# Dividing by the sum of dispatch weights behind the experts, with the token logits, norms, late weight tiles and gates in other places: one fused kernel (windowed attention, soft mixture of experts, routed mixture of experts) on one core

## The chip, the core and the metric

The kernel runs on one core of a Trainium2 chip. The core has a matrix engine (TensorE; PE in the views, and PEld for its weight loads), three elementwise engines (VectorE or DVE, ScalarE or ACT, GpSimd or POOL) and SyncE (SP), whose instruction queue starts nearly all transfers between HBM and the on-chip memory. Each engine works through its own queue strictly in order, and engines wait for each other by semaphores. Matrix products are written into eight PSUM banks of 128 x 512 fp32 values, from which ACT and DVE copy them on.

The metric is the device time of one execution in microseconds. For a comparison with the kernel before, several rounds are run on the same chip.

## What is computed

The reference chains three parts over 3,072 tokens of width 512. Cut to what matters here:

```python
# 1. attention with 4 sink keys and a window of 128 -> x [3072, 512]
# 2. soft mixture of experts: 8 experts, 4 slots each (32 slots)
logits = x @ phi
d = np.exp(logits - logits.max(0)); d /= d.sum(0) + 1e-09        # over tokens, per slot
slot_input = (d.T @ x).reshape(8, 4, 512)
for e in range(8):
    slot_out[e] = np.maximum(slot_input[e] @ w1[e], 0.0) @ w2[e]
c = np.exp(logits - logits.max(1)); c /= c.sum(1) + 1e-09         # over slots, per token
x = c @ slot_out.reshape(32, 512)
# 3. routed mixture of experts: every token goes to the best of 8 by cosine
logits = xn @ en.T / tau          # xn, en: rows divided by their norms
out = gate * (np.maximum(x @ w1[best], 0.0) @ w2[best])
```

Because `relu` passes a positive factor through, a positive division of `slot_input` by `d.sum(0)` can be done before the two weight products of an expert or behind them.

## The kernel before, in words

**Attention** (lines 201 to 520). 48 units (16 head pairs, 3 units each) are put into one order by a table of numbers (`KEYS`). The change does not touch it. Its last products are the token logits of the last head pair (`emit_f`, L369), added into `lt_all` (96 rows: 3 groups of 32 slots; 4 batches; 256 tokens) by DVE at L390.

**The mixture** (`mixture`, from L616) is a set of generators, each cut into steps. What order they run in stands in the string `ORDER` (L1410 and following): every name in it is one step of one generator, and each step puts its instructions at the end of its engine's queue. The names that matter:

- `wgt`, `scale`, `shift`: the maximum over the last batch and the rest, exponentials `e_sb`, their transpose `et_sb`, the common shift `a96`, the weight `wgt`, the running sum `s_run`. `scale` multiplies sum and weight, adds the 3 groups with a product against `rr96` (L700), and makes `rw = rsel * wgt / (sum + 1e-9)` (L702 to L705).
- `sum0`, `sum1` (two column halves of d.T @ x, L713, gathered into `si_acc` at L716); `in0`, `in1`: `si_acc` times `rw` (L723), copied into `sit`, the transposed slot inputs (L725).
- `f00` to `f13`: first weight products, `f<group of 4 experts><quarter of 512 inputs>` (L834); `t00` to `t11` relu and transposes; `v0`, `v1` second products (L858), `tu0`, `tu1` their transposes into `sot` and `ems` (L865 to L883).
- `tok0`, `tok1`: token logits back to rows of tokens, `c_tok` (L751 to L772; half of them by a copy `lt0` in the tile of `xtok`); `comb` their softmax over slots; `tot` the sum of c over tokens; `p0` to `p5` and `s0` to `s5` split and transpose c into `cs_t` (`cstack`).
- `norm`: 1 / (norm * tau) of the 8 expert embeddings (L731 to L746).
- `ch`: the likeliest expert, from `sot` x `ems`, then x `ccol`, then a maximum (L891 to L904). With its index SP starts the loads of that expert's two weights (L993, L995). `route`, `logit`, `cmp`, `gate`: routing logits, maxima, norms and gates of all tokens. `q0` to `q3` (L1021): slot outputs times the chosen expert's first weight.
- `T` (L1192) with `c0` to `c47`: 48 products, and on each a test that counts signs, 28 on ACT (L1201) and 20 on DVE (L1203). `ca`, `cb`, `e`, `gat`, `row`, `fetch` then pick the few hidden units whose sign is mixed and fetch their rows of the second weight by an indirect DMA. `D` (L1228) full products for 2 token tiles, `y2` to `y23` (L1375) four products for each of the other 22, `st` the scaled copies and stores (L1234, L1236).
- `K` and `J` are products whose result nobody reads. They keep PE busy: 25 `K` and 19 `J`, all 25 `K` ahead of `f00`.

**Weights and their tiles.** The 16 blocks of 2 MB expert weights go through the tiles `w0` to `w8` and a few others. Blocks 0 to 3 feed `f00` to `f03`, 4 to 7 feed `v0`, 8 to 11 feed `f10` to `f13`, 12 to 15 feed `v1`. Blocks 0 to 10 are loaded during attention. Blocks 11 to 15 each wait in SP's queue until an older tile has been read:

```python
for i in range(11, 16):
    load_w(i, wp, f"w{max(0, i - 11) + (i > 11)}", split=(i == 15))   # w0, w2, w3, w4, w5
```

Later tiles reuse the same tags: `cstack` in `w1`, `room` (scratch of `cmp` and `gate`) and then `sel` in `w3`, `junk` (scratch of the sign tests) in `w4`, `w2h` in `w5`.

## Time and profile before

| what | us |
|---|---|
| runs of the kernel (three) | 283.7, 287.44, 288.27; median 287.44 |
| the profiled execution, whole | 286.0 |
| its span, from the first to the last instruction | 284.3 |
| PE busy | 265.9 (94%) |
| DVE busy | 194.3 (68%) |
| ACT busy | 192.7 (68%) |
| POOL busy | 161.4 (57%) |

The profile is one execution. Its span leaves out 1.7 us around the first and the last instruction. A busy share is an average over stages that have different limits, so the stages are read one by one, from views that list instructions in order of time with what ended the idle time ahead of them. The granted clock of PE is given as a share of its full 2.4 GHz, so 1.00 is the upper and 0.50 the lower of its two levels.

### The profile page before, as it was taken

What the parts mean: (1) busy time and instruction counts of PE and PEld (TensorE: products, weight loads), DVE (VectorE), ACT (ScalarE), POOL (GpSimd) and SP (SyncE); (2) the same over time, 40 slices, a digit from 0 to 9 for tenths busy, and PEclk for the clock granted to TensorE, in tenths of its full rate; (3) what the DMA queues carried; (4) which work ended last, traced back from release to release, by engine and by line L of the source; (5) the groups of instructions that cost most, each with busy time, mean ns of one, the idle gap of its engine ahead of it and who ended that gap; (6) DMA issues with size and microseconds to landing.
All of it is one profiled execution on the core that took longest, in us unless ns stands there. A gap on an engine that the chain in (4) does not pass through costs nothing. (4 is left out here: it accounts for less than half of the span.)

```text
span 284.3 us, 8839 instructions
## 1 busy us (share of the span) xinstructions
PE 265.9 (94%) x3252; PEld 167.8 (59%) x3252; DVE 194.3 (68%) x573; ACT 192.7 (68%) x676; POOL 161.4 (57%) x375
## 2 busy tenths in 40 slices
PE   7987999979999989999999999989999999999992
PEld 5654666545666655666656563324277766577881
DVE  6887888988888988789986141383423999656420
ACT  2677989869799697898978510241124899775982
POOL 3488999978789788899798430001200999020000
PEclk9999999999999999999999999999999999999999
DMA  7939976198463795976807497999309400024785
GB/s 211 330 130 395 387 282 207 35 419 347 137 261 115 265 417 187 322 262 225 327 1 297 142 425 262 403 348 367 129 25 397 170 1 1 2 74 110 265 324 195
DMA packets 15053, 65.37 MB, mean 230 GB/s; under 512 B 2720, under 2 KB 2976, under 8 KB 11424
## 3 DMA queue, kind: packets, MB, share of 16 engines
q1 hardware_dynamic: 13456, 63.77, 60.1%
q10 hardware_dynamic: 1392, 0.48, 0.8%
q8 instruction: 27, 0.44, 0.6%
q0 software_dynamic: 160, 0.52, 0.6%
q14 instruction: 18, 0.15, 0.1%
HBM read 58.48 MB, written 6.29 MB: 228 GB/s over the span
## 5 line engine op out<-in xcount | busy, mean ns | idle before, releaser
L261 ACT ACTIVATE pr<-sc,nm 128x132 f32<-128x132 f32 x192 | 68.7, 375 | 8.4 <-DVE rs L266 3.4
L271 POOL TENSOR_TENSOR pr<-pr,rs 128x528 f32<-128x528 f32 x48 | 51.5, 1073 | 22.4 <-DVE rs L267 17.3
L261 ACT ACTIVATION_READ_ACCUMULATOR pr<-sc,nm 128x1 f32 x192 | 40.3, 210 | 0.0
L224 PE MATMUL sc<-qk 64*32 64x164 f32 (+4 forms) x1536 | 36.8, 295 | 0.3 <-ACT pr L261 0.2
L239 DVE COPY_PREDICATED sc<-t_le_q,sc 128x512 f32<-128x512 uint32 x48 | 33.1, 689 | 3.5 <-PE sc L224 2.0
L295 ACT ACTIVATE raw<-m 128x512 f32<-128x512 f32 x48 | 29.0, 604 | 7.9 <-PE xb L324 4.3
L247 DVE TENSOR_REDUCE sc<-sc 128x4 f32<-128x528 f32 x48 | 33.7, 703 | 0.8
L290 PE MATMUL m<-ident,pr 128*128 128x128 f32 x192 | 30.2, 279 | 4.3 <-ACT xtok L379 2.1
L301 POOL TENSOR_SCALAR_AFFINE_SELECT pt<-raw 128x512 f32<-128x512 f32 x48 | 30.6, 639 | 1.9 <-ACT raw L295 1.9
L345 PE MATMUL xa<-pt,v 128*64 128x256 f32 (+1 forms) x256 | 30.3, 360 | 0.0
L290 PEld LDWEIGHTS m<-ident,pr 128*128 128x128 f32 x192 | 21.4, 141 | 12.5 <-POOL pr L271 3.5
L224 PEld LDWEIGHTS sc<-qk 64*32 64x32 f32 x1536 | 21.4, 107 | 10.8 <-issue 4.7
L813 POOL CAST scr<-scr 128x256 fp32r<-128x256 f32 x6 | 2.4, 401 | 35.1 <-DVE scr L809 34.4
L345 PEld LDWEIGHTS xa<-pt,v 128*64 128x64 f32 x256 | 15.4, 136 | 8.4 <-issue 4.6
L308 POOL TENSOR_SCALAR_AFFINE_SELECT pt<-raw 128x256 f32<-128x256 f32 x48 | 19.6, 409 | 0.0
L345 PE MATMUL xb<-pt,v 128*64 128x128 f32 (+1 forms) x192 | 18.9, 314 | 0.0
L1169 POOL TENSOR_TENSOR w2h<-w2t,ones 128x512 fp32r<-128x512 f32 x8 | 8.4, 1056 | 16.3 <-DMA w2t<-in_m2w_dram 16.3
L379 ACT ACTIVATE xtok<-m 128x512 f32<-128x512 f32 (+1 forms) x32 | 15.7, 499 | 2.0 <-PE m L362 1.7
L1375 PE MATMUL b<-w2c,hm 128*128 128x512 f32 x54 | 17.0, 397 | 0.0
L362 PE MATMUL m<-ident,xt 128*128 128x128 f32 x96 | 15.9, 276 | 0.0
L345 PEld LDWEIGHTS xb<-pt,v 128*64 128x64 f32 x192 | 11.6, 136 | 7.3 <-POOL st L281 2.5
L1234 ACT ACTIVATE ot<-b,gsel 128x512 f32<-128x512 f32 x19 | 12.4, 687 | 3.3 <-PE b L1228 1.4
(354 smaller groups left out, 572.7 us busy)
## 6 DMA issues: line engine op xcount, KB each, us to landing
w<-in_m1w_dram SPq DMA_DIRECT2D x19, 1024.0 KB, 7.7
qk<-in_qkv_dram SPq DMA_DIRECT2D x15, 780.0 KB, 4.2
w<-in_m1w_dram SPq DMA_DIRECT2D x4, 2048.0 KB, 9.0
v<-in_qkv_dram SPq DMA_DIRECT2D x16, 448.0 KB, 5.0
out_dram<-ot SPq DMA_DIRECT2D x20, 256.0 KB, 3.4
x<-in_m1w_dram SPq DMA_DIRECT2D x4, 1024.0 KB, 8.1
w1t<-in_m2w_dram SPq DMA_DIRECT2D x4, 512.0 KB, 5.6
w2t<-in_m2w_dram SPq DMA_DIRECT2D x4, 512.0 KB, 8.3
```

Of the source, the lines that this page charges most:

```text
L224: pe.matmul(sc[r0:r0 + 32, h, o + lo:o + hi], lhsT=lhsT, rhs=qk[hp:hp + 64, k0 + lo:k0 + hi], start=True, stop=True)
L239: dve.copy_predicated(mv[:, :, :, 0:128], mk.to_broadcast([128, 2, 2, 128]), bv[:, :, :, 124:252])
L247: dve.tensor_reduce(mx, mv[:, :, :, 0:UW], axis=X, op=ALU.max, negate=True)
L261: act.activation(out=pr[:, h, i2, :], in_=mv[:, h, i2, 0:UW], func=AF.Exp, bias=nm[:, h, i2:i2 + 1], scale=0.125, accum_out=sm[:, h, i2, 0:1])
L271: pool.tensor_tensor(out=pr, in0=pr, in1=sm.rearrange("p h (i o) -> p h i o", o=1).to_broadcast([128, 2, 2, UW]), op=ALU.mult)
L290: pe.transpose(ps[:, h, i2, :], pr[:, h, i2, 0:128], ident)
L295: act.activation(out=raw, in_=tp_t.pop(u), func=AF.Copy)
L301: pool.affine_select(out=pt[:, :, :, 0, :], in_=raw_t[u], pattern=[[0, 2], [0, 2], [1, 128]], compare_op=ALU.is_ge, fill=0.0, base=0, chan ...
L308: pool.affine_select(out=pt_t[u][:, :, 0, 1, :], in_=raw_t[u][:, :, 1, :], pattern=[[0, 2], [-1, 128]], compare_op=ALU.is_gt, fill=0.0, ba ...
L345: pe.matmul(o[64 * h:64 * h + 64, c0:c0 + 128 * (l1 - l0)], lhsT=v[:, j, h, :], rhs=mv[:, h, 128 * l0:128 * l1], start=False, stop=last, s ...
L362: pe.transpose(ps[:, 128 * t:128 * t + 128], xt[:, 128 * (t0 + t):128 * (t0 + t) + 128], ident)
L1375: pe.matmul(y, lhsT=a, rhs=b, start=(k == 0), stop=(k == 3))
```

## The change

1. **Sum divided out later.** `rw` is now `rsel * wgt` alone. The sum is brought into the layout of the experts' outputs by two products against a table `rsl` (filled by POOL) and inverted into `rinv`; `tu0` and `tu1` multiply by it while they copy the outputs out of PSUM. `rr96` goes.
2. **Token logits and norms ahead.** `tok0`, `tok1` and the first steps of `norm` stand ahead of the first weight product. The token logits no longer need the copy `lt0`. `sit` is copied by ACT instead of DVE.
3. **Choice of the expert** by one group of eight products: c's sum over tokens is spread to 128 rows (`ccb`), multiplied into the outputs and summed on DVE (`mtm`, `mt`), instead of two products with a copy between.
4. **Other tiles for late loads**: blocks 11 to 15 go to `w0` to `w4` (before `w0, w2, w3, w4, w5`), `cstack` to `w5`, `w2h` to `w1`, `room` beside `junk` in `w4`.
5. **Gates behind the sign tests**: three of the five `gate` steps move from between the tests to behind the last `e6`, the other two behind `gat`.
6. **Warm-ups**: 25 `K` become 13 (6 ahead of `f00`), 19 `J` become 12. `s0` and `s1` move behind `v1`.
7. **The last token tile** is multiplied, copied and stored in two halves of 256 columns.

The diff, cut (the new `ORDER` is shown by its rows below; the parts for inputs of other kinds are left out):

```diff
-    rr96 = const.tile([96, 3, NS], F32, name="rr96")
...
+        rsl = sb.tile([96, 2, 4, NS], F32, name="rsl")
+        rinv = sb.tile([128, 2], F32, name="rinv")
+        ccb = sb.tile([128, NS], F32, name="ccb")
+        mtm = sb.tile([128, 4, 16], F32, name="mtm")
+        mt = sb.tile([128, 2, 4], F32, name="mt")
...
+            dve.tensor_scalar(out=rw, in0=rsel, scalar1=wgt, scalar2=None, op0=ALU.mult)
...
-            pe.matmul(tp[0:96, 256:257], lhsT=rr96.rearrange("p g s -> p (g s)"), rhs=s96, start=True, stop=True)
-            yield
-            dve.tensor_scalar(out=s96, in0=tp[0:96, 256:257], scalar1=1e-9, scalar2=None, op0=ALU.add)
+            for g in range(2):
+                pe.matmul(tp[:, g:g + 1], lhsT=rsl[:, g].rearrange("p j s -> p (j s)"), rhs=s96, start=True, stop=True)
+            yield
+            dve.tensor_scalar(out=rinv, in0=tp[:, 0:2], scalar1=1e-9, scalar2=None, op0=ALU.add)
             give(tp)
-            dve.reciprocal(out=s96, in_=s96)
-            dve.tensor_scalar(out=rw, in0=rsel, scalar1=wgt, scalar2=s96, op0=ALU.mult, op1=ALU.mult)
+            dve.reciprocal(out=rinv, in_=rinv)
...
-            dve.tensor_copy(sit[:, 2 * n:2 * n + 2, :, 0:SPE], ps[:, 2 * NS * n:2 * NS * n + 2 * NS].rearrange("p (c e s) -> p c e s", c=2, e=E))
+            act.activation(out=sit[:, 2 * n:2 * n + 2, :, 0:SPE], in_=ps[:, 2 * NS * n:2 * NS * n + 2 * NS].rearrange("p (c e s) -> p c e s", c=2, e=E), func=AF.Copy)
...
-            for k in range(2):
-                pe.transpose(tp[:, 32 * k:32 * k + 32], lt0[:, k, 128 * b2:128 * b2 + 128], ident[0:32, 0:32])
+            for b in range(2):
+                for k in range(2):
+                    pe.matmul(tp[64 * b:64 * b + 64, 32 * k:32 * k + 32], lhsT=lt_all[:, 2 * b2 + b, 64 * k:64 * k + 64], rhs=ident[0:96, 0:32], start=True, stop=True)
...
-            act.activation(out=so_sb[:, 0:256], in_=so[:, 0:256], func=AF.Copy)
+            act.activation(out=so_sb[:, 0:256], in_=so[:, 0:256], func=AF.Copy, scale=rinv[:, g:g + 1])
...
-            for c in range(4):
-                pe.matmul(ps[0:NS, 0:E], lhsT=sot[:, c], rhs=ems[:, c, 0:E], start=(c == 0), stop=(c == 3))
-            yield
-            dve.tensor_copy(e32[:, 0:E], ps[0:NS, 0:E])
...
-            pe.matmul(ps[0:1, 0:E], lhsT=ccol, rhs=e32[:, 0:E], start=True, stop=True)
+            for g in range(2):
+                for c in range(4):
+                    pe.matmul(ps[0:1, 0:E], lhsT=mt[:, g, c:c + 1], rhs=ems[:, c, 0:E], start=(g == 0 and c == 0), stop=(g == 1 and c == 3))
...
-        load_w(i, wp, f"w{max(0, i - 11) + (i > 11)}", split=(i == 15))
+        load_w(i, wp, f"w{i - 11}", split=(i == 15))
...
-        wgt wgt scale K K K K K K K K K K K K K K K K shift shift wgt wgt K K K shift shift shift scale scale sum0 sum0 sum1 scale scale K K K K in0 sum1 in0
+        wgt wgt scale tok0 tok1 norm shift shift wgt wgt norm K K K K shift shift scale shift shift sum0 sum0 sum1 tok0 in0 sum1 in0 K K f00 f00 in1 in1 f01
```

Line numbers in the views are those of the kernel before, and in the rows of the changed kernel its own.

On PE, from the end of attention to the first products with expert weights. `st` rows are warm-ups, `lt_all` the token logits, `nml` and `r` belong to `shift`, `e_sb` to `wgt`, `et_sb` products are `sum0` and `sum1`, `rr` is the old sum. Before:

```order
L1159 MATMUL b_3231<-st_135 128x192 x16
L677 MATMUL b_3248<-ident,nml 1x96
L668 MATMUL b_3252<-ident,e_sb 128x96 x2
L1159 MATMUL b_3231<-st_135 128x192 x3
L684 MATMUL b_3259<-ident,r_3214 96x1
L713 MATMUL b_3265<-xtok,et_sb 32x256 x6
L713 MATMUL m<-xtok,et_sb 32x256 x6
L700 MATMUL m<-s_3211,rr_139 96x1
L1159 MATMUL b_3231<-st_135 128x192 x4
L723 MATMUL b_3287<-rw,si_acc 128x32 x2
```

The same place in the changed kernel:

```order
L757 MATMUL b_3235<-ident,lt_all 64x32 x4
L761 MATMUL b_3235<-ident,lt_all 128x96 x4
L757 MATMUL b_3244<-ident,lt_all 64x32 x4
L761 MATMUL b_3244<-ident,lt_all 128x96 x4
L678 MATMUL b_3255<-ident,nml 1x96
L669 MATMUL b_3259<-ident,e_sb 128x96 x2
L738 MATMUL b_3263<-esq,ones 128x32
L1162 MATMUL m<-st_135 128x192 x4
L685 MATMUL m<-ident,r_3216 96x1
L716 MATMUL b_3274<-xtok,et_sb 32x256 x6
L716 MATMUL b_3282<-xtok,et_sb 32x256 x6
L726 MATMUL b_3292<-rw,si_acc 128x32 x2
```

The token logits and the norm's product stand where warm-ups stood, and the product of the sum between `sum1` and `in0` is gone from here.

On PE, from the last second product to the choice of the expert (`scr` rows are `s` steps, `cstack` rows are `J`, `so_sb` rows `tu1`). Before:

```order
L858 MATMUL b_3485<-w_3205,hT 32x256 x8
L820 MATMUL b_3553<-ident,scr 128x128 x4
L1161 MATMUL b_3231<-cstack 128x512
L874 MATMUL b_3559<-ident,so_sb 128x128 x2
L874 MATMUL m<-ident,so_sb 128x128 x2
L1161 MATMUL b_3231<-cstack 128x512 x2
L891 MATMUL m<-ems,sot 32x8 x4
L1161 MATMUL b_3231<-cstack 128x512
L897 MATMUL b_3574<-e_3141,ccol 1x8
L1161 MATMUL b_3231<-cstack 128x512 x6
```

In the changed kernel:

```order
L858 MATMUL b_3470<-w_3202,hT 32x256 x8
L820 MATMUL m<-ident,scr 128x128 x4
L1162 MATMUL m<-st_135 128x192 x3
L874 MATMUL b_3548<-ident,so_sb 128x128 x2
L874 MATMUL b_3549<-ident,so_sb 128x128 x2
L1162 MATMUL m<-st_135 128x192 x4
L896 MATMUL b_3563<-ems,mt 1x8 x8
L820 MATMUL b_3593<-ident,scr 128x128 x4
L1164 MATMUL m<-cstack 128x512 x2
L910 MATMUL b_3644<-ems,sot 32x40 x4
```

One group of eight products (L896) stands for the two groups L891 and L897, and two `s` steps stand behind `v1`, where there was one.

On DVE, behind the sign tests, from the last positions (`pos`) to the row numbers of the fetch (`ii`) and the end of the gates. Before:

```order
L1261 SCALAR_TENSOR_TENSOR pos<-b_4011,mix 128x3
L1271 TENSOR_SCALAR sel<-ki,pos 128x256 x2
L1300 TENSOR_SCALAR ebase<-em 128x1
L1303 TENSOR_SCALAR ii<-b_4035,ebase 128x1 x2
L1294 COPY cnt<-m 128x1
L969 TENSOR_REDUCE gate<-z 128x24
```

In the changed kernel:

```order
L1265 SCALAR_TENSOR_TENSOR pos<-b_4007,mix 128x3
L1275 TENSOR_SCALAR sel<-ki,pos 128x256 x2
L957 SCALAR_TENSOR_TENSOR junk<-z,iom 128x192
L958 TENSOR_REDUCE idx<-junk 128x24
L962 TENSOR_SCALAR n_3145<-n_3145 128x24
L963 RECIPROCAL n_3145<-n_3145 128x24
L964 TENSOR_TENSOR z<-z,n_3145 128x192
L1304 TENSOR_SCALAR ebase<-em 128x1
L1307 TENSOR_SCALAR ii<-b_4037,ebase 128x1 x2
L1298 COPY cnt<-b_4016 128x1
L968 TENSOR_REDUCE gate<-z 128x24
```

The five gate instructions stood between sign tests and now stand ahead of `ii`.

## Rows read from the trace of the kernel before

**Rows 1.** Stretches: us, length, busy of PE, PEld, DVE, ACT, POOL, clock, DMA.

```profile
163.24:170.01 6.77, 6.32 (x60) 4.83 (x60) 3.50 (x14) 1.42 (x5) 2.64 (x10) 1.00 1.01 425
170.01:206.69 36.68, 34.68 (x317) 12.44 (x318) 15.17 (x41) 7.07 (x18) 2.85 (x8) 1.00 0.77 299
206.69:215.75 9.06, 9.06 (x68) 7.16 (x69) 2.25 (x20) 2.28 (x6) 0.00 (x0) 1.00 0.35 124
220.34:244.28 23.94, 23.16 (x113) 16.06 (x109) 22.70 (x73) 22.11 (x72) 19.79 (x19) 1.00 0.13 51
...
254.49:278.69 24.20, 24.09 (x105) 19.10 (x104) 9.44 (x27) 19.85 (x32) 0.00 (x0) 1.00 0.68 230
```

**Rows 2.** Timeline, 164 to 172 us: start, us, engine, line, what [idle before, releaser].

```profile
164.96 0.09 PEld L677 LDWEIGHTS b<-ident,nml 96*1 96x1 f32 x1
...
166.92 1.04 PE L713 MATMUL m<-xtok,et_sb 128*32 128x256 f32 x12
167.16 0.48 DVE L716 SCALAR_TENSOR_TENSOR si_acc<-si_acc,all,b 96x256 f32<-96x256 f32 x1 [0.34 <-PE b L713]
...
168.64 0.30 DVE L705 TENSOR_SCALAR rw<-rsel,wgt,s 96x32 f32<-96x32 f32 x1
...
169.00 0.63 PE L723 MATMUL b<-rw,si_acc 96*128 96x32 f32 x4 [0.24 <-DVE rw L705]
...
170.01 1.92 PE L834 MATMUL b<-w,sit 128*32 128x512 f32 x16
```

**Rows 3.** Timeline, PE between the first weight product and the choice.

```profile
173.06 0.38 PE L735 MATMUL b<-esq,ones 128*128 128x32 f32 x2 [0.57 <-DVE esq L732]
...
173.37 3.64 PE L834 MATMUL b<-w,sit 128*32 128x512 f32 x32
...
176.94 0.31 PE L757 MATMUL m<-ident,scr 32*128 32x32 f32 x2
...
177.66 1.92 PE L834 MATMUL b<-w,sit 128*32 128x512 f32 x16
...
191.06 0.16 PE L798 MATMUL b<-ones,csum 128*32 128x1 f32 x1 [0.87 <-DVE en L743]
...
197.53 0.66 PE L820 MATMUL m<-ident,scr 128*128 128x128 f32 x4
```

**Rows 4.** Stretches of 2 us in which the DMA engines were not filled.

```profile
172.00:174.00 2.00, 1.43 (x14) 0.97 (x18) 0.87 (x6) 0.00 (x0) 0.00 (x0) 1.00 0.75 139
...
200.00:202.00 2.00, 2.00 (x24) 0.93 (x24) 1.46 (x7) 0.40 (x2) 0.40 (x1) 1.00 0.54 225
```

**Rows 5.** From the last second product to the chosen expert's weight (third: tile w1t).

```profile
206.05 0.64 PE L858 MATMUL b<-w,hT 128*32 128x256 f32 x8 [0.56 <-ACT so_sb L865]
...
210.93 1.96 SPq L993 DMA_DIRECT2D w1t<-in_m2w_dram  x4
...
DMA to landing us min/median/max: 3.9/5.6/6.7
```

**Rows 6.** Timeline, the gate's instructions among the sign tests.

```profile
226.04 0.65 DVE L958 SCALAR_TENSOR_TENSOR room<-z,iom 128x192 f32<-128x192 f32 x1
...
227.91 0.22 ACT L961 ACTIVATE n<-n 128x24 f32<-128x24 f32 x1 [0.63 <-DVE n L953]
...
233.98 1.18 DVE L965 TENSOR_TENSOR z<-z,n 128x192 f32<-128x192 f32 x1
```

**Rows 7.** Timeline, from the last sign test to the fetched rows.

```profile
244.28 1.28 ACT L967 ACT_TABLE_LOAD   x1
...
245.58 0.36 ACT L967 ACTIVATE z<-z 128x192 f32<-128x192 f32 x1
...
249.75 0.34 DVE L1303 TENSOR_SCALAR ii<-b,ebase 128x1 int32<-128x1 f32 x2 [2.84 <-PE b L1287]
...
253.80 0.63 ACT L1310 ACTIVATE w2c<-w2g 128x512 fp32r<-128x512 f32 x1 [0.86 <-DMA w2g<-in_m2w_dram,ii]
```

**Rows 8.** Stretch behind the last product, with PE idle.

```profile
283.00:284.30 1.30, 0.00 (x0) 0.00 (x0) 0.00 (x0) 0.00 (x0) 0.00 (x0) 0.50 0.00 0
```

More of the change, by code (lines that the diff above doesn't have):

```diff
@@ L1 @@
-from itertools import islice
 from contextlib import ExitStack
@@ L797, in total @@
             ps = take()
-            pe.matmul(ps[0:NS, 0:1], lhsT=csum, rhs=ones[:, 0:1], start=True, stop=True)
+            pe.matmul(ps[:, 0:NS], lhsT=ones, rhs=csum, start=True, stop=True)
             yield
-            dve.tensor_copy(ccol, ps[0:NS, 0:1])
+            dve.tensor_copy(ccb, ps[:, 0:NS])
             give(ps)
@@ L938, in compare @@
         def compare():
-            room = tiles["room"] = wp.tile([128, NTILE * (NS + E)], F32, tag="w3", name="room")
+            room = tiles["room"] = P.compared()
             qt = room[:, 0:NTILE * NS].rearrange("p (t x) -> p t x", t=NTILE)
@@ L1240, in stores @@
         for t in range(NTILE):
-            store(t)
-            yield
+            for c in (slice(0, DM),) if t < NTILE - 1 else (slice(0, 256), slice(256, 512)):
+                store(t, c)
+                yield
     def classify(fs):
@@ L1401, in kernel_body @@
     ORDER = """
-        wgt wgt scale K K K K K K K K K K K K K K K K shift shift wgt wgt K K K shift shift shift scale scale sum0 sum0 sum1 scale scale K K K K in0 sum1 in0
-        K K f00 f00 in1 in1 norm norm norm tok0 f01 f01 f02 f02 tok0 tok0 tok0 f03 f03 tok1 tok1 tok1 t00 t01 f10 f10 t00 t00 t01 t01 comb comb comb norm comb
-        comb comb tot norm f11 f11 f12 f12 v0 v0 f13 f13 t10 t11 tot tot v0 v0 v0 t10 t10 t11 t11 v0 v0 v0 v0 p0 p0 p0 s0 s0 v1 p1 p1 p1 v1 tu0 tu0 tu0 tu0
-        tu0 tu0 tu0 tu0 p2 p2 p2 v1 p3 p3 p3 v1 p4 p4 p4 v1 p5 p5 p5 v1 v1 v1 tu1 v1 tu1 s1 J tu1 tu1 J tu1 tu1 J ch ch J ch J J ch ch tu1 tu1 s1 const late J
@@ L1414, in kernel_body @@
-        st flag x5 y18 y18 st m5 y17 y17 y17 y17 y20 y18 y19 m5 st flag st flag y19 y19 y19 st hint y20 y20 y21 y20 y21 st y21 y21 y22 st y22 y22 y22 st y23 y23 y23 y23 st
+        wgt wgt scale tok0 tok1 norm shift shift wgt wgt norm K K K K shift shift scale shift shift sum0 sum0 sum1 tok0 in0 sum1 in0 K K f00 f00 in1 in1 f01
+        f01 tok1 tok0 tok1 scale f02 f02 comb comb scale comb f03 f03 scale norm t00 t01 f10 f10 t00 t00 t01 t01 comb comb norm comb tot norm f11 f11 f12 f12
+        v0 v0 f13 f13 t10 t11 v0 v0 tot tot v0 t10 t10 t11 t11 v0 v0 v0 v0 p0 p0 p0 v1 p1 p1 p1 v1 tu0 tu0 tu0 tu0 tu0 tu0 tu0 tu0 tu0 tu0 p2 p2 p2 v1 p3 p3
```

80 lines of the change are left out of this document (44 added, 36 removed).

## Prediction

> **What bounds the kernel now.** I read the stretches first, to see which engine is full in each part behind attention, which the change leaves alone. From the last copy of token logits to `f00` (163.24 to 170.01) PE is busy for 6.32 of 6.77 us, but part of that is warm-ups, so busy time settles nothing there. From `f00` to the end of the weight products (170.01 to 206.69) it is busy for 34.68 of 36.68, nearly all real work: each microsecond of PE work or PE wait taken out counts. Around the choice (206.69 to 215.75) it is busy all the time, again padded. During the sign tests (220.34 to 244.28) DVE and ACT are both full, with 22.70 and 22.11 of 23.94 us. From 254.49 PE is full (24.09 of 24.20) until its last product at 278.69 [rows 1].
>
> Then the timeline, to see which wait ends last in the stretches that busy time leaves open. Ahead of `f00`, DVE makes `rw` (168.64, 0.30 us), and the products of `in0` wait for that until 169.00. The first half of `si_acc` had been there at 167.16 + 0.48 = 167.64. So the division by the sum is the chain that ends last [rows 2].
>
> **Ahead of `f00`.** Without the sum, `rw` needs only `wgt`, and `in0` waits for the half of `si_acc` at 167.64 and for `sum1` ahead of it on PE. With the small chain behind it unchanged (169.00 to 170.01, `f00` follows 1.01 later [rows 2]), the most that can come is 169.00 - 167.64 = 1.36 us by DVE; on PE `sum1` ends at 166.92 + 1.04 = 167.96 [rows 2], so 1.04: bound 1.05. On the other side, `tok0` and `tok1` now stand ahead of the transpose at 164.96 [rows 2], in place of 16 warm-ups. A set is 4 small products and 4 transposes of 96 columns. Two small ones took 0.31, four of 128 columns 0.66 [rows 3]: 0.62 + 0.41 = about 1.0 us a set, the second figure interpolated. Two sets from about 163.2 end at 165.3, some 0.3 late, of which wgt's chain has slack for half. At 1.5 a set, which nothing here reaches, the transpose would be 1.3 late and the gain nothing. I take 0.9, bounds 0 to 1.05. The copy of `sit` changes to ACT, which is nearly idle (1.42 of 6.77 us [rows 1]); if its queue is late there, the lower bound has it.
>
> **From `f00` to the end of `v1`.** Five things leave PE here.
> - The pause behind `f00`, 170.01 + 1.92 to 173.37, is filled by `in1`, the norm's product and a wait of 0.57 for `esq` [rows 3]. Both norm and wait have moved ahead: 1.0.
> - `tok0` and `tok1`, at 176.94 to 177.66 the first of them [rows 3]: 0.72 each, 1.44.
> - New: two products for `rinv`, like the 0.16 product of `tot` [rows 3]: minus 0.25.
> - The wait of 0.87 ahead of `tot`, on the norms (191.06 [rows 3]). These are ready long before now. Its product now spreads to 128 rows and takes 0.2 longer: 0.65.
> - `s0`, 0.66 at 197.53 [rows 3], overlapped by its neighbours: 0.58 goes behind `v1`, where warm-ups make room.
>
> Together 1.0 + 1.44 - 0.25 + 0.65 + 0.58 = 3.4. Bounds: 2.6, if behind `f00` the wait of 0.57 alone goes and the two sum products cost twice as much with a wait; 3.6, if they cost nothing.
>
> This holds only if the weights come earlier too. `f00` starting 0.9 and `v1` 3.4 sooner means that the last block must land sooner. The queue for blocks 11 to 15 runs dry while it waits for tiles: at 172 to 174 the DMA engines are 75% busy, and at 200 to 202 54%, where the last block comes in [rows 4]; 0.54 of 2 us puts its end at about 201.1. With tiles `w0` to `w4` each block waits for the very next product (`f00`, `f01`, `f02`, `f03`, `v0`), so those holes close. Blocks 12 to 15 are each released by a product one place earlier in the row than before and that row starts 0.9 sooner, so I estimate the last landing at 197 to 198, and `v1`'s last products, 0.9 + 3.4 - 0.6 sooner than now, want it near 199.5. What `cstack`, `w2h` and `room` do in their new tiles is hidden: their old readers end before the new writers start. Without this cover, 2 us would go back.
>
> **The choice.** The critical line runs from the end of `v1` to the load of `w1t`, issued at 210.93, with landings 3.9 to 6.7 us later [rows 5], then `q0` at 215.75, where the stretch ends [rows 1]. The chain ahead of the issue has one product group and one copy less, but a product with `ccb` and a sum on DVE more; I count 0.15 for it. PE has 7 warm-ups less and `s0`, `s1` more: about 0.4 shorter. The first tile landed at 210.93 + 3.9 = 214.83, 0.9 ahead of `q0`, so a shorter PE line is not stopped by it yet. I take 0.4, bounds -0.2 (the extra DVE steps cost more than they save) and 0.6.
>
> **Sign tests and gates.** The gate's DVE steps, the first at 226.04 (0.65), the last at 233.98 (1.18), are five with 2.9 us together; on ACT a step of 0.22 waits 0.63 for DVE [rows 6]. Taken out of the tests, DVE falls to 19.8 us and ACT becomes the bound, at 22.11 - 0.22 busy in 23.94 less its wait: about 1.1 earlier, bounds 0 and 1.5. Behind the tests the 2.9 us stand ahead of `ii`, which now waits for 2.84 us for PE, then starts at 249.75 [rows 7]. They just fill that pause, so `ii` is 0.2 late at most against the tests' end: 0.9 net. Queued behind them are `ebase`, `ii` and so the fetch; `w2c` at 253.80 ends its 0.86 us wait on it [rows 7]. Also, the load of the exponential's table, 1.28 us at 244.28 [rows 7], moves behind `gat`'s and the fetch's issue, to where ACT waits for the fetch. I take 0.9, bounds 0 (DVE late by what the tests gained) and 1.4.
>
> The next activation starts at 245.58, 0.02 behind the table's load [rows 7]: loading is all that it costs here. The Trainium skill ("ScalarE: Activation LUTs", "What ACT_TABLE_LOAD costs") puts a drain of some 1.38 us beside a load of about 1.28. The trace agrees on the load and shows no drain. By the page this stage would gain 0.3 instead of 0.9, and the sum would be 0.6 less, as an estimate.
>
> **The last tile.** The halves let a first copy start earlier, but both lie in one PSUM bank; a copy from the other half of a bank in use waited for PE (0.56 us at 206.05 the other way round [rows 5]). ACT's copy of 512 columns is near 0.63 (as that of `w2c` [rows 7]), and the second half's store is the last. Nearly nothing: 0.1, bounds -0.2 and 0.4. What comes behind the last data is a fixed end.
>
> **Sum.** 0.9 + 3.4 + 0.4 + 0.9 + 0.1 = 5.7. Each wait removed leaves neighbours closer, and some small wait comes back; I take off 0.4, an allowance and no reading: 5.3. The profiled run took 286.0, the median is 287.44 and the runs lie between 283.7 and 288.27, 4.6 us apart. I lay the gain on 286.7, the middle of those two: **281.4 us**.
>
> **The rivals.**
> *The gain is given back.* The weights land as late as before (2.0 back), or `q0` stands until `w1t` lands, or the gates delay the fetch (1.1). For: DMA at 0.54 at 200 to 202 shows that the tail of the weights is thin already [rows 4]. Against: blocks now wait for earlier readers. One or two of these leave 1.5 to 4: 282.7 to 285.2, that is, no change. This holds the rival that the new tiles don't do what they are meant to.
>
> *More than the sum.* The upper bounds add up to 1.05 + 3.6 + 0.6 + 1.4 + 0.4 = 7.05, and the weights might have held more than I saw: 279.6 or a little lower.
>
> *PE's clock falls: slower.* There are 12 `K` and 7 `J` fewer, and only 6 `K` stand ahead of `f00`. If PE falls to its lower level of 1.2 GHz there, the first weight products run at half rate: `f00` to `f03` are 1.92 + 3.64 + 1.92 = 7.48 us [rows 2, 3], so 7.5 more: 281.4 + 7.5 = 288.9. It decides against the change from 5.3 us of such work at half rate, and by more than 2% from about 11. Against it: the clock is 1.00 in every stretch of work [rows 1, 4], and falls to 0.50 only in the stretch behind 283.00, with PE idle since 278.69 [rows 1, 8]. Real products (the token logits) stand where most of the warm-ups ahead of `f00` stood. The Trainium skill ("TensorE: Matmul & The Clock Gate", "What's actually happening") says that activity lets the throttle go and idleness brings the lower level back, which speaks against taking warm-ups out. By that rule, it would be this rival's time.
>
> **How the numbers follow.** A change of 2%, 5.75 us, is about what a measurement of this kernel can tell from none; the border is 281.7. Chances: the sum as worked out, gain 4 to 7, 0.68 (0.40 faster, 0.28 same, since 5.3 of 286.7 lies at the border); given back 0.20 (same); more than the sum 0.07 (faster); the clock 0.05 (0.04 slower, 0.01 same). Faster 0.47, same 0.49, slower 0.04. The range goes from the sum's upper bound with the room of the runs below it (278.8) to the end of the given-back case (285.2): outside lie the clock and the thinnest ends, 0.15 together.
>
> **What would show it.** Right: `f00` near 169.0; `v1` ending near 202 without PE waits over 0.5 on weights; `w1t` issued near 206.2 and `q0` near 211; sign tests of about 22.8 us from the first to the last, with ACT full and DVE not; `w2c` near 248; clock 1.00 throughout. Wrong: a matmul on `w` that waits for DMA from 190 to 202 (tiles); `q0` released by `w1t` (choice); `ii` released by DVE's gate rather than PE (gates); a stretch from 165 to 178 with a clock near 0.5 (warm-ups).

## The result

The changed kernel takes 282.23 us against 286.26 us (medians of 20 runs each). The ratio is 0.9852, 95% interval 0.9815 to 0.9889: 4.2 us less (3.2 to 5.3). That is faster beyond what the interval leaves open, and within the 2% that the chances called "same". 281.4 us had been forecast, in a range of 278.8 to 285.2. The ratio is taken over the runs of either kernel that lie within 1.5% of its fastest; the medians are of all 20.

The profiled execution of the changed kernel took 281.05 us, with a span of 279.3 (284.3 before). Its stretches, cut at the same events as in [rows 1], and ahead of them the one of the kernel before that starts at the last token logits (columns as in [rows 1]):

```profile
162.87:170.01 7.14, 6.69 (x65) 4.89 (x60) 3.87 (x14) 1.42 (x5) 2.64 (x10) 1.00 1.01 425
```

```profile
161.98:168.05 6.07, 5.98 (x71) 4.04 (x65) 3.85 (x14) 1.96 (x9) 3.09 (x12) 1.00 1.01 425
168.05:201.49 33.44, 32.79 (x303) 11.56 (x304) 14.94 (x41) 6.64 (x15) 2.87 (x8) 1.00 0.83 342
201.49:209.92 8.43, 8.43 (x79) 7.17 (x79) 2.58 (x22) 2.99 (x7) 0.00 (x0) 1.00 0.37 123
214.51:238.20 23.69, 22.85 (x113) 16.08 (x109) 21.33 (x68) 21.91 (x71) 19.67 (x19) 1.00 0.15 61
248.48:272.94 24.46, 24.36 (x108) 19.46 (x108) 9.45 (x27) 19.84 (x32) 0.00 (x0) 1.00 0.66 222
```

The first three stretches are 1.07, 3.24 and 0.63 us shorter. The stretch of the sign tests is hardly shorter, and the one of the last products is 0.26 longer. Laid beside the terms of the prediction, all of them as differences of the two profiled executions:

| place | foreseen | measured |
|---|---|---|
| start to the last token logits (attention) | 0 | 0.89 |
| from there to `f00` | 0.9 | 1.07 (7.14 to 6.07) |
| `f00` to the end of `v1` | 3.4 | 3.24 (36.68 to 33.44) |
| end of `v1` to `q0` | 0.4 | 0.63 (9.06 to 8.43) |
| `q0` to `w2c` | 0.9 | 0.17 (38.05 to 37.88) |
| `w2c` to PE's last product | 0 | -0.25 (24.89 to 25.14) |
| behind PE's last product | 0.1 | -0.75 (5.61 to 6.36) |
| sum | 5.7, less 0.4 | 5.00 |

Without attention, whose products the change doesn't touch, 4.11 us are left, which agrees with the 20 runs. The 0.89 can't be told from chance: over the fourteen profiled executions of this study, with the same order of attention, its last token logits started anywhere between 160.81 and 166.13 us. A single profiled execution can therefore not show a difference of a few us in the whole time. The stretches behind attention can: the stretch from `f00` to `v1` was 33.44 or 33.45 us in all nine kernels that had the changed order there, and 36.67 or 36.68 in the three with the old one. The experiments are read from them.

The new head of the chain, in the timeline of the changed kernel (start, us, engine, line, what, [idle before, releaser]):

```profile
161.98 0.94 DVE L386 TENSOR_TENSOR lt_all<-lt_all,m 96x256 f32<-96x256 f32 x2 [5.49 <-ACT xtok L375]
...
167.04 0.63 PE L726 MATMUL b<-rw,si_acc 96*128 96x32 f32 x4
...
168.05 1.07 PE L834 MATMUL m<-w,sit 128*32 128x512 f32 x8
```

`in0` starts 5.06 us behind the token logits, where it was 169.00 - 162.87 = 6.13 [rows 2], and `f00` again 1.01 us behind it.

### The profile page after: what moved, and what is told of

Its sections match the earlier page's. It is cut to its first block, busy times and chain, and to the rows that moved or that the text cites. A ratio compares the mean times of both kernels' runs of the same rounds, so it can differ in the third digit from the quotient of the medians.

```text
span 279.3 us, 8848 instructions
## 1 busy us (share of the span) xinstructions
PE 262.2 (94%) x3257; PEld 166.3 (60%) x3257; DVE 194.1 (69%) x574; ACT 193.4 (69%) x679; POOL 162.0 (58%) x377
## 4 chain that ended last, share of the span: by engine, by line
PE 57%; DVE 16%; POOL 10%; DMA 6%; issue 5%; ACT 4%; SPq 0%; POOLq 0%; ACTq 0%; DVEq 0%
PE sc L220 5%; PE b L858 5%; POOL pr L267 5%; PE m L286 4%; PE xa L341 4%; PE b L834 4%; DVE sc L243 3%; PE b L1195 3%; PE b L1385 3%; PE m L358 3%; PE xb L341 3%; DMA out_dram<-ot 2%; PE m L365 2%; DVE sc L235 2%; PE m L417 2%
## 5 line engine op out<-in xcount | busy, mean ns | idle before, releaser
L1204 ACT ACTIVATE junk<-b 128x512 f32<-128x512 f32 (+1 forms) x26 | 14.8, 568 | 0.7 <-PE b L1195 0.3
L1385 PE MATMUL b<-w2c,hm 128*128 128x512 f32 x45 | 14.7, 400 | 0.0
```

The source lines that it names most:

```text
L1385: pe.matmul(y, lhsT=a, rhs=b, start=(k == 0), stop=(k == 3))
```

## The experiments

Lengths in us from the profiled execution of each kernel; "logits" is the start of the last token logits on DVE. The ratio to the kernel before is of timed runs on the same chip, with its 95% interval.

| kernel | logits to `f00` | to end of `v1` | to `q0` | first sign product to `ii` | behind PE's last product | ratio |
|---|---|---|---|---|---|---|
| before | 7.14 | 36.68 | 9.06 | 29.40 | 5.61 | |
| changed | 6.07 | 33.44 | 8.43 | 29.05 | 6.36 | 0.985 (0.982 to 0.989) |
| x_tile | 6.07 | 33.44 | 8.42 | 29.20 | 5.77 | 0.986 (0.979 to 0.993) |
| x_w2 | 6.07 | 33.44 | 8.42 | 29.55 | 6.66 | 0.978 (0.969 to 0.987) |
| x_gates | 6.06 | 33.44 | 8.43 | 29.63 | 6.19 | 0.991 (0.986 to 0.996) |
| x_tags | 6.06 | 33.44 | 8.43 | 29.08 | 6.30 | 0.981 (0.972 to 0.990) |
| x_nowarm | 5.82 | 33.44 | 7.80 | 28.81 | 6.06 | 0.994 (0.990 to 0.998) |
| x_tok | 5.84 | 35.49 | 8.43 | 29.04 | 6.11 | 0.992 (0.986 to 0.997) |
| x_sum | 5.81 | 33.45 | 8.42 | 29.48 | 5.73 | 0.982 (0.976 to 0.988) |
| x_sum41 | 5.81 | 33.45 | 8.42 | 29.47 | 6.03 | 0.985 (0.978 to 0.992) |
| x_best | 5.82 | 33.44 | 8.42 | 29.12 | 5.57 | 0.985 (0.979 to 0.991) |
| x_nosum | 6.67 | 36.67 | 9.06 | 29.16 | 5.27 | 1.013 (1.004 to 1.022) |
| x_nosum2 | 6.05 | 37.50 | 9.05 | 29.22 | 5.24 | (one run) |
| x_rr | 7.15 | 36.67 | 9.08 | 29.26 | 5.71 | 1.011 (0.999 to 1.024) |

The ratios of the experiments rest on 4 to 10 runs each and carry attention's scatter, so small differences between them are not read here. The stretch to `ii` scatters too: it is 29.04 to 29.20 us in the five kernels with the changed order of the sign tests and warm-ups behind `v1` (changed, x_tile, x_tags, x_tok, x_best), and 29.16 to 29.40 in the four with the old order (before, x_nosum, x_nosum2, x_rr), 0.16 apart on the mean.

### Is it the division that held `f00`? (x_nosum, x_nosum2)

```diff
+            dve.tensor_scalar(out=rw, in0=rsel, scalar1=wgt, scalar2=None, op0=ALU.mult)
...
-            dve.tensor_scalar(out=rw, in0=rsel, scalar1=wgt, scalar2=s96, op0=ALU.mult, op1=ALU.mult)
...
-        shift shift shift scale scale sum0 sum0 sum1 scale scale K K K K in0 sum1 in0 K K f00
+        shift shift shift scale shift sum0 sum0 sum1 in0 sum1 in0 K K K K scale scale scale K K f00
```

In x_nosum2 the new line reads `shift shift shift scale shift sum0 sum0 sum1 in0 sum1 in0 K K f00 f00 in1 in1 scale scale scale`.

> The kernel before with one edit: rw is made without the division, which is left out altogether (outputs lack the division by the sum), with the sum's product behind in0. Theory: the division was the chain that ended last ahead of f00, so f00 comes 0.9 to 1.05 us sooner behind the last token logits (7.14 us before), and the whole time falls by about as much. Rival 'PE or the second half of si_acc ends last': less than 0.4 us.

The expectation was missed: `f00` came 0.47 us sooner, not 0.9. The timeline of PE shows why:

```profile
168.23 0.63 PE L725 MATMUL m<-rw,si_acc 96*128 96x32 f32 x4
...
168.70 0.67 PE L1161 MATMUL b<-st 128*128 128x192 f32 x4
...
169.31 0.33 PE L702 MATMUL b<-s,rr 96*96 96x1 f32 x2
...
169.88 1.50 PE L836 MATMUL b<-w,sit 128*32 128x512 f32 x12
```

With the logits at 163.21, `in0` started 5.02 us behind them, 1.11 sooner than before. But I had put four warm-ups and the sum's product between `in0` and `f00`, and these stood in `f00`'s way: here warm-ups on PE were not free. Its ratio above one goes with no stretch behind attention that is longer than before; I have no cause for it but attention's scatter, and that was not settled.

> The kernel before without the division by the sum (left out, outputs lack it), as x_nosum, but with nothing between in0 and f00 that was not there before: the sum's product stands behind in1 and the four warm-ups that stood ahead of in0 are left out. In x_nosum, in0 started 1.1 us sooner behind the last token logits (5.02 against 6.13 us), but f00 only 0.47 us, behind warm-ups and the sum's product that had been put there. Theory: f00 now comes 1.0 to 1.1 us sooner than in the kernel before (6.05 to 6.15 us behind the last token logits instead of 7.14), as in the changed kernel (6.07). Rival 'something else holds f00': 6.5 us or more.

With nothing new in between, `f00` starts 6.05 us behind the logits, as in the changed kernel (6.07):

```profile
163.39 0.94 DVE L390 TENSOR_TENSOR lt_all<-lt_all,m 96x256 f32<-96x256 f32 x2 [5.50 <-ACT xtok L379]
...
169.44 1.93 PE L836 MATMUL b<-w,sit 128*32 128x512 f32 x16
```

So the division, with the sum's product and the four warm-ups that stood ahead of `in0`, was worth the 1.07 us. The division alone was not: in the kernel before, those warm-ups ended at 168.75, 0.25 ahead of `in0`, so with them in place no more than that could come. The stretch behind `f00` grew to 37.50, where the sum's product now stood on PE's path.

### Where do the 3.2 us behind `f00` come from? (x_tok)

```diff
-        wgt wgt scale tok0 tok1 norm shift shift wgt wgt norm K K K K shift shift ... tok0 in0 sum1 in0 K K f00 f00 in1 in1 f01 f01 tok1 tok0 tok1
+        wgt wgt scale K K K K K K K K shift shift wgt wgt K K K K shift shift ... in0 sum1 in0 K K f00 f00 in1 in1 norm norm tok0 f01 f01 tok0 tok0 tok1 tok1 tok1
```

> The changed kernel with the token logits and the norm's first steps back behind the first weight product and warm-ups in their old place (8 more K). Theory of the prediction: f00 stays 6.07 us behind the last token logits, or comes 0.1 us earlier, and the stretch from f00 to the end of v1 grows from 33.4 by 2.1 (two sets of token logits at 1.0 us) plus the norm's product and wait (up to 0.9), so 2.1 to 3.0 us. Rival 'PE has slack there that hides them': it grows by less than 1 us.

The stretch grew by 2.05 us, just under the 2.1 to 3.0 expected. PE's timeline, token logits and the norm's product among the first weight products:

```profile
174.29 0.39 PE L738 MATMUL b<-esq,ones 128*128 128x32 f32 x2
174.61 0.43 PE L757 MATMUL b<-ident,lt_all 96*64 96x32 f32 x8
174.97 0.55 PE L761 MATMUL b<-ident,lt_all 96*128 96x96 f32 x4
...
177.31 0.43 PE L757 MATMUL m<-ident,lt_all 96*64 96x32 f32 x8
177.67 0.55 PE L761 MATMUL m<-ident,lt_all 96*128 96x96 f32 x4
```

A set takes about 0.84 us (174.61 to 175.45, where `f01` starts), the norm's product 0.3 with no wait in front of it: 2 x 0.84 + 0.32 = 2.0. PE has no slack there, so what is taken out counts in full. (Attention ended late in this execution, at 166.13 us, but the clock is 1.00 from there on.) `f00` came 0.23 us sooner than in the changed kernel, where 0 to 0.1 was expected, about as it does without warm-ups (x_nowarm, 0.25): token logits, the norm's product and four warm-ups together seem a little more than the place ahead of it holds.

### Did the new tiles bring the weights in time? (x_tags)

```diff
-        load_w(i, wp, f"w{i - 11}", split=(i == 15))
+        load_w(i, wp, f"w{max(0, i - 11) + (i > 11)}", split=(i == 15))
```

(with `cstack` back in `w1` and `w2h` in `w5`)

> The changed kernel with the late weight blocks 11 to 15 back in the tiles w0, w2, w3, w4, w5 (and the tiles of cstack and w2h back as before; the scratch of cmp stays beside junk). Theory 'the weights must come earlier for the gain': the last products of v1 wait for DMA and the stretch from the first weight product to the choice, 33.4 us from f00 to the end of v1, grows by 1 to 2 us. Rival 'the transfer was hidden anyway': no PE wait on a weight, the stretch within 0.2 us of 33.4.

The rival is right: 33.44 us, to the hundredth. The DMA columns (last three: clock, share, GB/s) of the two kernels at the end of the loads, the changed one first:

```profile
194.00:196.00 2.00, 2.00 (x20) 0.71 (x16) 0.88 (x7) 0.40 (x2) 0.00 (x0) 1.00 1.01 426
196.00:198.00 2.00, 2.00 (x24) 0.65 (x20) 1.90 (x8) 0.00 (x0) 0.86 (x3) 1.00 0.25 102
```

```profile
196.00:198.00 2.00, 2.00 (x24) 0.62 (x20) 1.90 (x8) 0.00 (x0) 0.83 (x3) 1.00 0.44 184
```

The loads end near 196.5 with the new tiles and near 196.9 with the old, where they ended near 201.1 before [rows 4]. The new tiles are worth 0.4 us of transfer time, and nothing waits for it. What brought the last block some 4 us sooner (0.9 of them from attention) is that the products that free the tiles came sooner. With the same tiles, SP issued these loads at 172.00, 177.07, 179.65, 188.53 and 193.08 us in the kernel before, each behind a wait for PE, and at 170.07, 174.20, 176.59, 184.62 and 188.05 in x_tags: 1.9 us sooner for the first, 5.0 for the last.

### Warm-ups and the clock (x_nowarm)

```diff
-        ... norm K K K K shift shift scale ... in0 K K f00 ... tu1 s0 K K K tu1 tu1 s0 K K tu1 tu1 K K ch ch s1 tu1 tu1 J ch ...
+        ... norm shift shift scale ... in0 f00 ... tu1 s0 tu1 tu1 s0 tu1 tu1 ch ch s1 tu1 tu1 ch ...
```

(and so on, no `K` and no `J` is left)

> The changed kernel without any of the 25 warm-up products left behind attention (13 K and 12 J). Theory 'the clock holds': granted clock 1.00 from 160 to 215 us, f00 within 0.3 us of its place behind the last token logits (6.07 us), and q0 up to 0.9 us earlier at most, since w1t's first piece then comes last. Rival 'clock': the granted clock falls to 0.5 in some stretch between 162 and 178 us and the first weight products take up to 7 us longer.

Ahead of `f00` the clock held at 1.00 in the profiled execution, and `f00` came 0.25 us sooner. At the choice, both theories had a part. Without `K` and `J` there, `q0` comes 0.63 us sooner, and it stands until `w1t` lands:

```profile
207.87 0.64 PE L1022 MATMUL b<-w1t,sot 128*32 128x256 f32 x8 [1.38 <-DMA w1t<-in_m2w_dram]
```

And then the clock falls, as the stretches around it show (PE busy first, clock third from the end):

```profile
200.00:205.00 5.00, 4.54 (x54) 3.64 (x51) 2.37 (x21) 2.09 (x6) 0.00 (x0) 1.00 0.05 13
205.00:208.00 3.00, 1.62 (x18) 1.52 (x21) 0.20 (x1) 0.72 (x2) 0.00 (x0) 1.00 0.88 299
208.00:214.40 6.40, 6.40 (x44) 4.20 (x40) 2.40 (x8) 2.13 (x5) 1.28 (x2) 0.62 1.02 405
```

Behind 3 us with PE busy for 1.62, the granted clock over the next 6.4 us is 0.62, so a good part of them ran at 1.2 GHz. From `q0` to the first sign product it takes 6.57 us instead of 4.59. The sum of the two is 14.37 against 13.02: these warm-ups earn 1.35 us in these two executions. This agrees with the rule cited ahead ("TensorE: Matmul & The Clock Gate" of the Trainium skill): idleness brings the lower level back. The rival of the falling clock was a real one, only at another place than where I had set it, and 7 `K` and 9 `J` between `v1` and `q0` are still enough there. The ratio of x_nowarm (0.990 to 0.998) lies above that of the changed kernel (0.982 to 0.989), though from the logits to the end its profiled execution is only 0.5 us longer (117.8 against 117.3). That execution was the fastest of its ten runs and had the highest mean clock (0.986; the others 0.969 to 0.982), so the clock may have fallen further, or elsewhere, in the others; that is not shown.

### What the sign tests gave (x_gates, x_w2, x_sum, x_sum41)

The gates' five steps left the tests, yet DVE is busy for 21.33 of 23.69 us and not for the 19.8 foreseen. Three small DVE instructions, 128 x 5 elements, have grown; each ends with an instruction of POOL (timeline of the changed kernel):

```profile
230.28 1.29 POOL L1173 TENSOR_TENSOR w2l<-w2t,w2h 128x512 fp32r<-128x512 f32 x1
...
230.39 1.20 DVE L1253 SCALAR_TENSOR_TENSOR ac<-ac 128x5 f32<-128x5 f32 x1
...
231.52 0.88 POOL L1187 TENSOR_TENSOR gtf<-gt 128x128 f32<-128x128 f32 x2
...
231.63 0.39 DVE L1254 TENSOR_SCALAR allp<-ac 128x5 f32<-128x5 f32 x1
...
232.05 0.37 DVE L1255 SCALAR_TENSOR_TENSOR mix<-ac,allp 128x5 f32<-128x5 f32 x1
...
233.72 0.69 DVE L1206 TENSOR_SCALAR_CACHE_REDUCE junk<-b 128x512 f32<-128x512 f32 x1 [0.49 <-PE b L1195]
```

In the kernel before, the same three (L1249 to L1251) took 0.17 us each, and there the gate's product `z` x `n` took 1.18 [rows 6], behind a POOL instruction that ran beside it:

```profile
233.66 1.29 POOL L1170 TENSOR_TENSOR w2l<-w2t,w2h 128x512 fp32r<-128x512 f32 x1
```

Behind the tests, with POOL idle, that product takes 0.36:

```profile
241.78 0.36 DVE L964 TENSOR_TENSOR z<-z,n 128x192 f32<-128x192 f32 x1
```

All five gate steps take 1.54 us there (0.35, 0.35, 0.18, 0.30, 0.36), where they took 2.86. So about half of the "2.9 us of gate work" was DVE standing still inside an instruction, which the profile counts as busy. The three sums grew by 1.45, and that closes the account of DVE's busy time: 22.70 - 2.86 + 1.45 = 21.29, measured 21.33. Counted from the first sign product, DVE reaches the sums at 15.88 us instead of 17.79, 1.91 sooner, and leaves them only 0.46 sooner. x_gates puts the gates back:

```diff
-        ... q3 D T i cmp T T c13 c9 c11 ... c25 c22 c24 ... cb cb e7 e5 ... e6 gate gate gate gat ... gate row
+        ... q3 D T gate i cmp T T c13 c9 gate c11 ... c25 c22 gate c24 ... cb cb gate e7 e5 ... e6 gat ... row
```

> The changed kernel with the five gate steps back at their old places among the sign tests. Theory 'most of the gate's 2.9 us was waiting for POOL, and that wait has only moved': the product z x n takes about 1.2 us again and L1253 about 0.2 us, and the stretch from the first sign product to ii goes from 29.05 to about 29.4 us, 0.35 more. By the prediction's term (2.9 us of work, ACT the bound) it would go up by 1.1 us or more, with another exponential table load ahead of the fetch. Whole time: 0 to 0.5 us more by the first, 1 us by the second.

The wait goes back to where it was:

```profile
230.40 1.18 DVE L964 TENSOR_TENSOR z<-z,n 128x192 f32<-128x192 f32 x1
...
234.54 0.17 DVE L1253 SCALAR_TENSOR_TENSOR ac<-ac 128x5 f32<-128x5 f32 x1
```

and the stretch to `ii` is 0.58 us longer: above the 0.35 of the first theory, about half of the second's 1.1. It is also 0.23 to 0.47 longer than in the four kernels with the old order, and why is open. From DVE's last test to `ii` it is 5.43 us in all three kernels, so neither the exponential's table nor the gates on DVE lie on that path, wherever they stand.

x_w2 lets POOL do one split fewer ahead of the sums:

```diff
-        ... u0 c18 w2 w2 w2 u1 u1 c21 ... h u0 ca w2 T T T
+        ... u0 c18 w2 w2 u1 u1 c21 ... h u0 ca w2 w2 T T T
```

> The changed kernel with one edit: the seventh of POOL's eight splits of the second weight is issued behind the product gta instead of ahead of the sums gtf. Theory 'blocked by POOL': DVE's small instruction L1253 took 1.20 us in the changed kernel because POOL's L1173 ran until the same moment, and the next two 0.39 and 0.37 behind gtf; with POOL's queue shorter there, all three fall to about 0.17 to 0.2 us, DVE no longer waits 0.49 us for PE behind them, and the stretch from the first sign product to ii, 29.05 us, falls by 0.3 to 0.6 us (ACT is the bound then). Rival 'the instruction waits for ACT's last sign sum': L1253 stays near 1.2 us.

The gain is not there. L1253 to L1255 fall to 0.17 us each, as expected, but DVE's wait of 0.49 us for PE behind them stays (so it was not theirs), and the split that was moved now meets `sel`:

```profile
232.28 0.17 DVE L1253 SCALAR_TENSOR_TENSOR ac<-ac 128x5 f32<-128x5 f32 x1
...
235.58 1.04 POOL L1172 TENSOR_TENSOR w2h<-w2t,ones 128x512 fp32r<-128x512 f32 x1
...
235.73 2.39 DVE L1275 TENSOR_SCALAR sel<-ki,pos 128x256 fp32r<-128x256 f32 x2
...
236.70 1.27 POOL L1173 TENSOR_TENSOR w2l<-w2t,w2h 128x512 fp32r<-128x512 f32 x1
```

Two `sel` take 2.39 us, where they took 0.63. Counted from the first sign product, DVE reaches them 1.26 us sooner than in the changed kernel (19.31 against 20.57) and the next test 0.49 later (21.62 against 21.13), and the stretch is 0.5 us longer. x_sum moves the sums instead, behind two more tests, and x_sum41 also gives test 41 to DVE (both with a whole last tile and no warm-ups ahead of `f00`):

```diff
-        c34 ca c35 h u0 ca w2 T T T D D c37 c38 ca ca i
+        c34 c35 h u0 T T T D D c38 ca ca w2 c37 ca ca i
```

> The changed kernel with three edits that touch different stretches: the last token tile whole; no warm-ups ahead of f00 (6 K fewer, the 7 behind v1 stay); and DVE's first sums of signs (L1252 to L1256) moved behind two more sign tests, to where POOL has finished its split and its sums gtf and waits for these sums itself. Theory 'POOL blocks small DVE work whose place it shares': L1253 to L1255 fall to 0.17 to 0.25 us without any other DVE instruction growing by more than 0.3 us, and the stretch from the first sign product to ii, 29.05 us, falls by 0.2 to 0.4 us (ACT ends the tests then). Rival 'each place has its POOL work': the wait turns up in another instruction and the stretch stays within 0.1 us or grows. f00 comes 0.25 us earlier behind the last token logits (5.8 against 6.07 us) with the clock at 1.00, and 5.6 us lie behind PE's last product against 6.3. Whole time about 1 us below the changed kernel's.

> As x_sum, and sign test 41 is moved from ACT to DVE, which the theory says has room now: ACT's part of the tests, solid at 23.2 us, falls by 0.8, DVE's rises by 0.7. Theory: the stretch from the first sign product to ii falls by 0.6 to 1.1 us against the changed kernel's 29.05. Rival 'DVE is full as well': it stays at x_sum's value or rises by up to 0.7 us.

Again the three sums take 0.17 us in both, and in x_sum `sel` pays again:

```profile
234.88 0.17 DVE L1253 SCALAR_TENSOR_TENSOR ac<-ac 128x5 f32<-128x5 f32 x1
...
236.92 1.30 POOL L1173 TENSOR_TENSOR w2l<-w2t,w2h 128x512 fp32r<-128x512 f32 x1
...
237.10 1.53 DVE L1275 TENSOR_SCALAR sel<-ki,pos 128x256 fp32r<-128x256 f32 x2
```

The stretch is 29.48, 0.43 longer than in the changed kernel. In x_sum41 the first two `sel` take 0.72 us, but DVE has a test more (0.69), and ACT waits for PE instead (0.43 and 0.71): 29.47. In this stretch POOL is busy for 19.67 of 23.69 us, so such a DVE instruction is likely to meet it wherever it is put. The sign tests, which read PSUM, show no such growth (0.67 to 0.69 us for 512 columns).

The changed kernel without warm-ups shows the stretch when neither place is met. In x_nowarm POOL is 1.8 us ahead (its first split starts 1.40 us ahead of the first sign product, where it starts 0.42 behind it in the changed kernel), and the sums and `sel` are both short:

```profile
230.80 0.17 DVE L1253 SCALAR_TENSOR_TENSOR ac<-ac 128x5 f32<-128x5 f32 x1
...
234.25 0.61 DVE L1275 TENSOR_SCALAR sel<-ki,pos 128x256 fp32r<-128x256 f32 x2
```

DVE's last test then ends 23.02 us behind the first sign product (23.62 in the changed kernel, 23.97 before), ACT's last at 23.53, and the stretch is 28.81, the shortest of all, 0.35 to 0.59 below the kernels with the old order. It is no clean test, as the granted clock is 0.50 there from 214.44 to 216 us.

The Trainium skill has a rule for this ("SBUF — State Buffer", "SBUF: two separate sides"): DVE and GpSimd share a pair of ports under an exclusive lock. Of a GpSimd instruction and a DVE instruction in a two-port mode, or with two SBUF inputs against a GpSimd instruction that reads SBUF, the one that starts first has the ports for the whole instruction, and the other stands. The trace agrees for L1253, which has two SBUF inputs: 1.20 us instead of 0.17 beside a POOL instruction that ends 0.02 us earlier. L1254 and `sel` have one; whether they ran in a two-port mode, no row here shows.

### The last tile in halves (x_tile)

```diff
-            for c in (slice(0, DM),) if t < NTILE - 1 else (slice(0, 256), slice(256, 512)):
+            for c in (slice(0, DM),):
...
-            y21 y21 y22 st y22 y22 y22 st y23 y23 st st
+            y21 y21 y22 st y22 y22 y22 st y23 y23 y23 y23 st
```

> The changed kernel with its last token tile whole again (four products of 512 columns, one copy, one store). Theory 'halves cost': in the changed kernel ACT waits for all of PE's products before the first half, then needs two copies and SP two issues, so from PE's last product to the end of the span is 6.36 us, against 5.61 us before; whole, it falls back to 5.6 us, 0.7 us less, and the other stretches stay (first weight product to choice within 0.2 us). Rival 'halves help by 0.1, as predicted, and the long tail is chance': it stays at 6.2 to 6.5 us. The time of the whole kernel can hardly show 0.7 us.

Behind PE's last product it takes 5.77 us instead of 6.36. Over all kernels it is 6.06 to 6.66 with halves (six of them) and 5.24 to 6.03 with a whole tile (eight), with means of 6.28 and 5.62. ACT's last copies, first of the changed kernel, then of x_tile:

```profile
273.02 0.84 ACT L1237 ACTIVATE ot<-b,gsel 128x256 f32<-128x256 f32 x2 [0.26 <-PEq L1581]
```

```profile
273.42 0.69 ACT L1237 ACTIVATE ot<-b,gsel 128x512 f32<-128x512 f32 x1 [0.23 <-PEq L1588]
```

PE's products for the first half end at 272.46, those for the second at 272.94, and the first copy starts at 273.02, so it is no earlier than a whole one would be. Two copies take 0.84 us instead of 0.69, and SP's last issue ends 0.83 us behind the last copy, where it ends 0.45 behind in x_tile.

### The copy at the start (x_rr)

```diff
-    dve.tensor_copy(rr96, rsel.rearrange("p (a s) -> p a s", a=1).to_broadcast([96, 3, NS]))
...
+        pool.tensor_copy(rr96, rsel.rearrange("p (a s) -> p a s", a=1).to_broadcast([96, 3, NS]))
```

> The kernel before with one edit: the 0.25 us copy rr96 on DVE, ahead of attention, is made by POOL behind attention. In the changed kernel, without that copy, the first score product started 0.17 us earlier (5.86 against 6.03) and the last token logits of attention were 0.89 us earlier (161.98 against 162.87). Theory 'the copy was on the path': start at about 5.86 and the end of attention 0.2 to 0.9 us earlier. Theory 'chance': the first score product starts at 5.86 or 6.03 without regard to the copy, and the end of attention scatters between executions by more than 0.5 us.

The first score product started at 6.04 us, where it started at 6.03 in the kernel before. Over all kernels it started between 5.29 and 6.03 with the copy on DVE and between 5.41 and 6.05 without it. The end of attention came later, at 164.11. So nothing shows that the copy was on the path, and the 0.89 us of the profiled executions are not counted for the change.

### A version that keeps what helped (x_best)

> The changed kernel with two of the edits that helped their stretches, and its sign tests in the changed kernel's own order: the last token tile whole, and no warm-ups ahead of f00 (the 7 behind v1 and the 12 J stay). Theory: f00 5.8 us behind the last token logits (6.07 in the changed kernel), 33.4 us from f00 to the end of v1, 8.4 to q0, 29.0 to 29.2 us from the first sign product to ii, 5.6 us behind PE's last product (6.3), the clock at 1.00 until that: 0.9 us less than the changed kernel behind attention, which the whole time, with attention's scatter of some us, shows hardly. Rival 'clock': without warm-ups ahead of f00 it falls in some executions, and the first weight products take longer.

Behind attention it has 5.82, 33.44, 8.42, 29.12 and 5.57 us: from the logits to the end of the span 116.1 us, against 117.3 in the changed kernel and 121.4 before. The clock is 1.00 in the stretches behind attention. In whole time it is 1.5% below the kernel before (281.16 against 285.71 us), and its last 1.2 us over the changed kernel can't be told from chance there.

## Why the prediction was right, and where its steps were not

**Ahead of `f00`: right.** 0.9 foreseen, 1.07 measured, a hair above the upper bound of 1.05. x_nosum2 shows the cause: the division, with the product and the warm-ups ahead of `in0`. x_tok shows 0.23 us that the token logits and warm-ups ahead give back.

**`f00` to `v1`: right in size and in most of its parts.** 3.4 foreseen, 3.24 measured. Token logits and the norm's product give 2.05 by x_tok. In the traces, `f01` starts 2.42 us behind `f00` instead of 3.36 (0.94 for 1.0), and the old token logits took 0.72 and 0.71. The two products for `rinv` hold PE for 0.53 (174.04 to 174.57), not 0.25. The wait ahead of `tot` and `s0` were not tried alone. The step that failed is the one beside the sum: "Without this cover, 2 us would go back". The tiles cover nothing (x_tags). I had read the holes in the loads [rows 4] as caused by the tiles; they came mostly from late readers, and these moved by themselves.

**Choice: right, slightly more.** 0.4 foreseen, 0.63 measured, just over the upper bound of 0.6. The load of `w1t` was issued 3.88 us behind the end of `v1` (205.37), where it was 4.24 before [rows 5], so the new chain is 0.36 shorter and not 0.15.

**Sign tests and gates: the term that was wrong, 0.17 for 0.9.** The failed step is "Taken out of the tests, DVE falls to 19.8 us": it fell to 21.33. The 2.9 us were durations of busy rows, and about half of them (2.86 against 1.54) was waiting for POOL. Of my two rows one showed it: 1.18 us for 128 x 192 elements, where 0.65 stood for as many at L958 [rows 6], and POOL busy for 19.79 of 23.94 us [rows 1]. The wait moved to three instructions on the chain to `pos` and took back 1.45 of the 1.91 us that DVE had gained by then. ACT's part did end 0.63 us earlier, but `ii` follows DVE's last test, which came 0.35 earlier. The fetch took 0.19 longer from `ii` to `w2c`; over all kernels this lies between 4.04 and 4.24, so it can be chance. Even x_nowarm, where the sums and `sel` don't wait for POOL, gains no more than 0.59 by `ii`; whether the term was too large without that wait as well stays open, as its clock is low at the start of the stretch.

The exponential's table: 1.28 us, and the next activation 0.02 later, as before:

```profile
241.96 1.28 ACT L966 ACT_TABLE_LOAD   x1
...
243.26 0.36 ACT L966 ACTIVATE z<-z 128x192 f32<-128x192 f32 x1
...
243.56 0.34 DVE L1307 TENSOR_SCALAR ii<-b,ebase 128x1 int32<-128x1 f32 x2 [1.36 <-PE b L1291]
```

No drain shows, as before the change. But the load came ahead of the fetch's issue (244.07) and not behind it, as the prediction had it; the table was on no path to `ii`, and nothing shows a gain from moving it.

**The last tile: sign wrong, -0.75 for 0.1.** The mechanism, both halves held by PE, was in the text; what it costs was not. A second copy and a second store issue, 0.15 and 0.4 us, were priced at nothing. The means over all kernels put the whole cost at 0.66 us. Nor is what comes behind the last data a fixed end: from ACT's last copy to the end of the span it took 4.5 to 5.3 us with a whole tile and 5.1 to 5.7 with halves.

**The allowance of 0.4** stood for such things, and was too small by 1.2 (5.7 - 4.11 - 0.4). That the forecast is only 0.8 us below the median is owed to the large terms, which came about as foreseen, and by 0.4 us to luck: the baseline of 286.7 was that much above the later median. The forecast case (gain 4 to 7) is what came, at its lower end.

**The slower rival** didn't happen, and x_nowarm shows that it wasn't idle talk: at the choice, its profile shows PE's clock falling once all warm-ups are gone, at a price of 1.35 us.

## What to carry to other kernels

A busy row is not always work: before an instruction's duration enters a sum, hold it against rows of the same form, and look at what the other engines do at that moment, since such a wait can move with the work. What is taken out of the chain that ends last counts in full (2.05 and 1.07 us here), while the transfers that waited for readers needed no help here once the readers came sooner. Splitting the last piece of a pipeline can help only if its first half starts earlier; here it didn't, and the split added an instruction to each queue behind.
